# Bias-table groups, their loads and one tile size reordered in an attention-plus-MoE kernel

## The chip, the core and the metric

The kernel runs on one core of one Trainium2 chip. The metric is the device time of one execution in microseconds (us). The kernel before took 677.99 us, the median of 3 runs (677.85 to 678.35). Differences under about 0.2% (1.4 us) can't be told from no change here.

## The reference, cut to what matters

Attention with a learned position bias, over 4 batches, 8 heads, 576 positions and 64 values per head, feeds a mixture layer with a rational activation:

```python
scores = scale * np.matmul(q, k.transpose(0, 1, 3, 2))
psi_rel = np.log1p(np.abs(pos[:, None] - pos[None, :]))
psi_i = np.log1p(np.maximum(pos[:, None], 1.0))
h = np.maximum((psi_rel / psi_i)[..., None] @ w1 + b1, 0.0)   # 32 hidden
bias = h @ w2                                                 # one 576 x 576 table per head
attn = softmax(scores + bias.transpose(2, 0, 1))
x = (attn @ v).reshape(2304, 512)
hh = x @ w_in                                                 # 512 -> 2048
g = (a0 + a1*hh + a2*hh**2 + a3*hh**3) / (1 + |b0|*|hh| + |b1|*hh**2 + 1e-06)
out = g @ w_out                                               # 2048 -> 512
```

All is float32, and products of the mixture layer are made of a high and a low part of each operand (three matmuls in place of one).

## The kernel before, in words

**Table stage (0 to about 50 us).** The bias depends on the row position and the distance only, so it is built once, in 36 groups of 16 rows ("group n" holds rows 16n to 16n+15). For one group, VectorE (DVE) and ScalarE (ACT) make four relu rows in a ring of 18 buffers (line 614 on DVE, line 612 on ACT; how many of the four go to ACT depends on the group's width: none above 432 columns, one above 400, else two). TensorE (PE) multiplies them by the second weight (line 653, tile pb), ACT scales the result into a tile e (line 658, 8 buffers), and SyncE (SP) starts a DMA that writes it to a table in DRAM (line 664, tile tab). The relu rows are issued two groups ahead. The list `order` gives the order of the 36 groups; "place y" is a position in it, from 0 to 35.

Groups 0-7, 8-15, 16-23, 24-31 and 32-35 form blocks 0 to 4 of 128 rows (block 4: 64 rows). The function `load_bias(p, c)` (line 260) reads block c of head pair p back from DRAM into one row of a bias tile in SBUF with three DMAs (block 4: six, on 64 partitions each). It reads what line 664 wrote, so its first DMA waits in SP's queue until the block's last write has landed, and all that stands behind it in that queue waits with it. The dictionary `done` says after which place which block is loaded.

**Attention stage (about 46 to 270 us).** The work is cut into 72 steps. Step i computes scores of 128 rows for two heads on PE (line 337, tile sc), then DVE adds the bias and takes the minimum (line 347, two instructions a step; the first is row c of the bias tile of that step), ACT takes the exponential (line 363), PE transposes the result (line 406), ACT copies it (line 414), and PE multiplies by v (line 446). Two score tiles are shared by all steps, so PE can't begin the scores of a step before DVE has read those of the step before. The first steps, in order, use block 0, 1, 2 of unit 0, block 0, 1 of unit 1, then block 3 (step 5) and block 4 (step 6):

```python
steps = [(0, 0), (0, 1), (0, 2), (1, 0), (1, 1), (0, 3), (0, 4), (1, 2), (1, 3)]
```

The scores of steps 0 and 1 are issued at places 34 and 35 of the table stage (`EARLY = 2`). Unit 1's v is loaded by `load_v(1)` at place 21 and first used behind step 3. From step 4 on, weights are read and split into high and low parts in the gaps.

**Mixture stage (270 us to the end).** 48 steps of two matmul groups on PE: `x @ w_in` (line 313, tile h) and `g @ w_out` (line 787, tile o). Tiles of even token groups (xh, xl) lie in the pool xp on the right side of SBUF, those of odd token groups in a pool on the left side; of the four groups of weights in use, three lie in the pool wpool on the right side and the fourth (fp = 3) in a buffer of the bias pool, on the left.

The order on each engine is the order of the code (`tc.manual_schedule()`); no scheduler moves anything.

Of the kernel before, what the change touches and what calls it, by code (L numbers as in the profile page):

```python
# [8 lines left out]
F32 = mybir.dt.float32  # L9
# [7 lines left out]
P = 128  # L17
# [16 lines left out]
def tile_attn_moe(  # L34
# [14 lines left out]
    cpool = ctx.enter_context(tc.tile_pool(name="cpool", bufs=1))  # L49
# [16 lines left out]
    def tab_rows(c, h):  # L66
        n, w, o = P if c < 4 else 64, H * TW - 1, h * TW + S - 1 - P * c
        flat = tab[c].rearrange("r h x -> (r h x)")
        return flat[o:o + n * w].rearrange("(r w) -> r w", w=w)[:, :S]
# [11 lines left out]
        for d_, nm in ((woh, "woh"), (wol, "wol")):  # L81
            d_[g] = pool.tile([P, 2, DM], F32R, tag=f"{nm}{g}", name=f"{nm}{g}")

    fill = cpool.tile([P, 104], F32, tag="fill", name="fill")
    nc.gpsimd.memset(fill[:, 0:8], 0.0)
    stg = ctx.enter_context(tc.tile_pool(name="stg", bufs=2))
    bpool = ctx.enter_context(tc.tile_pool(name="bpool", bufs=2))
# [143 lines left out]
    with tc.manual_schedule():  # L231
# [3 lines left out]
        with ExitStack() as actx:  # L235
# [16 lines left out]
            def load_bias(p, c):  # L252
                if p not in bias:
                    bias[p] = bpool.tile([P, 10, S], F32, tag="bias", name=f"bias{p}")
                t = bias[p]
                r0, r1 = tab_rows(c, 2 * p), tab_rows(c, 2 * p + 1)
                for o, x, y, r in ((5 + c, 0, S, r1[:, 0:S]), (c, 64, S, r0[:, 0:512]), (c, 0, 64, r0[:, 512:S])):
                    n = P if c < 4 else 64
                    for z in range(0, P, n):
                        nc.sync.dma_start(out=t[z:z + n, o, x:y], in_=r)  # L260

            def load_qk(u, eng=nc.sync):
                p, b = units[u]
                q = qkp.tile([P, S], F32, tag="q", name=f"q{u}", bufs=3)
                k = qkp.tile([P, S], F32, tag="k", name=f"k{u}", bufs=3)
                eng.dma_start(out=q, in_=qt[b, p])
                eng.dma_start(out=k, in_=kt[b, p])
                qk[u] = (q, k)

            def load_v(u, eng=nc.sync):  # L270
                p, b = units[u]
                t = vpool.tile([P, 5, P], F32, tag="v", name=f"v{u}")
                eng.dma_start(out=t, in_=vp[b, p])
                vt[u] = t
# [292 lines left out]
            with ExitStack() as bctx:  # L567
                tpool = bctx.enter_context(tc.tile_pool(name="tpool", bufs=1, side="right"))
                rpool = bctx.enter_context(tc.tile_pool(name="rpool", bufs=8, side="right"))
                ring = [bpool.tile([P, 10, S], F32, tag="bias", name="ring")]  # L570
                ring = [ring[0][:, x, :] for x in range(10)]
                ring2 = tpool.tile([P, 8, S], F32, tag="ring2", name="ring2")
                ring += [ring2[:, x, :] for x in range(8)]
                lts = tpool.tile([P, S], F32, tag="lts", name="lts")
                bts = tpool.tile([P, NG * 4], F32, tag="bts", name="bts")
                LCUT = 320
                nc.scalar.dma_start(out=cs, in_=cst)
                nc.sync.dma_start(out=lts[:, :LCUT], in_=ltab[:, :LCUT])
                nc.sync.dma_start(out=lts[:, LCUT:], in_=ltab[:, LCUT:])
                for u in range(2):  # L580
                    load_qk(u)
                load_v(0)
                G.memset(qc, 1.0 + 1e-6)
                G.memset(wmin, -8.0 * 0x38000000)
                V.tensor_scalar(out=bts, in0=pts, scalar1=b1s, scalar2=None, op0=ALU.mult)
                A.activation(out=w28, in_=cs[:, 8 + 5 * NG:], func=AF.Identity, scale=8.0)
                for a, z in ((0, LCUT), (LCUT, S)):
                    V.tensor_scalar(
                        out=lts[:, a:z], in0=lts[:, a:z], scalar1=w1s, scalar2=None, op0=ALU.mult
                    )  # L590
                warm = ps_tp.tile([P, 2, 512], F32, tag="tp", name="warm")
                for x in range(9):
                    T.matmul(warm[:, 0, 0:P], ident, ident, start=True, stop=True)

                def dist(n):
                    return max(NROW * n + NROW, S - NROW * n)

                ENG = [
                    "DDDD" if dist(n) > 432 else "DDDA" if dist(n) > 400 else "DDAA" for n in range(NG)
                ]  # L600

                rows = {}
                LEAD, EARLY = 2, 2
                nring = [0]

                def relu(n):
                    for c, e in enumerate(ENG[n]):
                        r = ring[nring[0] % len(ring)][:, :dist(n)]
                        nring[0] += 1
                        m = 4 * n + c  # L610
                        if e == "A":
                            A.activation(out=r, in_=lts[:, :dist(n)], func=AF.Relu, bias=bts[:, m:m + 1])
                        else:
                            V.tensor_scalar(
                                out=r, in0=lts[:, :dist(n)], scalar1=bts[:, m:m + 1], scalar2=0.0,
                                op0=ALU.add, op1=ALU.max,
                            )
                        rows[n, c] = r

                bg = [w_job(f, z) for f in range(KF - LATE) for z in range(2)]  # L620
                after = {}
                for f in range(0 if wide else 6):
                    after[2 * f + 5] = [lambda f=f: [w_load(f, z) for z in range(2)]]
                after.setdefault(16, []).append(lambda: w_carve(3))
                for f in range(6, KH):
                    after[11 + f] = [lambda f=f: [w_load(f, z) for z in range(2)]]
                bg = in_order(bg, after)

                order = [16, 17, 0, 18, 1, 19, 2, 20, 3, 21, 4, 22, 5, 23, 6, 11, 7, 12]
                order += [8, 13, 32, 14, 33, 15, 34, 9, 35, 10, 31, 24, 30, 25, 29, 26, 28, 27]  # L630
                done = {16: 2, 19: 0, 30: 4, 31: 1}
                for n in order[:LEAD]:
                    relu(n)
                for y, n in enumerate(order):
                    if y == 21:
                        load_v(1)
                    if y + LEAD < NG:
                        relu(order[y + LEAD])
                    i0 = NROW * n
                    mid = i0 + NROW - 1  # L640
                    pool, nm = (ps_sc, "sc")
                    if y == NG - 1:
                        pool, nm = (ps_mx, "mx")
                    elif y % 3 == 1:
                        pool, nm = (ps_tp, "tp")
                    pa = pool.tile([P, 2, 512], F32, tag=nm, name=f"pb{n}")
                    cuts = sorted({0, mid, 512, EW})
                    for a, z in zip(cuts, cuts[1:]):
                        o = pa[:, a // 512, a % 512:a % 512 + z - a]
                        for c in range(4):  # L650
                            x = rows[n, c]
                            x = x[:, a - mid:z - mid] if a >= mid else x[:, mid - a:mid - z:-1]
                            T.matmul(
                                o[32 * c:32 * c + 32], w28[:, 32 * c:32 * c + 32], x,
                                start=True, stop=True,
                            )
                    e = rpool.tile([P, EW], F32, tag="e", name=f"e{n}")
                    A.activation(
                        out=e, in_=pa.rearrange("p a s -> p (a s)")[:, :EW], func=AF.Identity,
                        scale=rts[:, n:n + 1],  # L660
                    )
                    g, k = divmod(n, 8)
                    x0 = S - NROW - i0
                    nc.sync.dma_start(
                        out=tab[g][NROW * k:NROW * k + NROW, :, x0:x0 + EW].rearrange("r h x -> (r h) x"),
                        in_=e,
                    )
                    if y in done:
                        load_bias(0, done[y])
                    if y == NG - 1:  # L670
                        load_bias(0, 3)
                    if y >= NG - EARLY:
                        step_a(y - NG + EARLY)
                A.activation(out=babs, in_=abs_[:, 4:6], func=AF.Abs)
# [282 lines left out]
```

## Time and profile before

| | us |
|---|---|
| median of 3 runs | 677.99 (677.85 to 678.35) |
| the profiled execution, its own time | 679.69 |
| its span, first to last instruction | 677.9 |
| PE busy in the span | 667.6 (98%) |
| DVE busy | 570.6 (84%) |
| ACT busy | 481.9 (71%) |

The profiled execution is 1.70 us longer than the median of the runs, and 1.8 us of it lie outside the span. A row of a timeline gives the start and the length of a run of equal instructions and, in brackets, how long the engine was idle before it and what ended that. A row of stretches gives the length of the stretch and then, engine by engine, its busy time in it.

### The profile page before, as it was taken

How to read it: one execution, taken by the hardware profiler on the slowest of the kernel's cores; microseconds unless marked ns; L12 is line 12 of the kernel's file. 1: busy time of each engine (PE TensorE's matmuls, PEld its weight loads, DVE VectorE, ACT ScalarE, POOL GpSimd, SP SyncE). 2: the span in 40 equal slices, each digit the busy share in tenths (PEclk: the TensorE clock that was granted, in tenths of full speed). 3: DMA queues.
4: the chain of work that ended last, by engine and by line, in shares of the span. 5: the costliest groups of instructions: out<-in, count | busy, mean ns of one | idle time of the engine just before them, and what ended most of it. 6: DMA issues, size and time to landing. Idle time of an engine off the chain costs nothing.

```text
span 677.9 us, 16639 instructions
## 1 busy us (share of the span) xinstructions
PE 667.6 (98%) x6466; PEld 576.8 (85%) x6466; DVE 570.6 (84%) x1068; ACT 481.9 (71%) x769; POOL 156.5 (23%) x116
## 2 busy tenths in 40 slices
PE   9998999999999999999999999999999999999997
PEld 6766888888888888999999999999999999999995
DVE  7975788888888896699998989898978787878776
ACT  7976899998888997676676767676755555555561
POOL 0000034334333232122222222222222222222221
PEclk9998999999999999999999999999999999999999
DMA  6888488788788864223635353679721212122021
GB/s 241 287 303 304 159 279 275 224 284 258 245 262 291 270 217 141 98 81 115 221 98 203 90 191 99 199 217 358 251 104 47 94 47 93 47 94 94 1 94 46
DMA packets 74847, 119.01 MB, mean 176 GB/s; under 512 B 11905, under 2 KB 33809, under 8 KB 74769
## 3 DMA queue, kind: packets, MB, share of 16 engines
q1 hardware_dynamic: 74624, 117.79, 52.9%
q8 instruction: 51, 0.84, 0.5%
q14 instruction: 28, 0.22, 0.1%
q10 hardware_dynamic: 144, 0.16, 0.1%
HBM read 79.17 MB, written 35.61 MB: 169 GB/s over the span
## 4 chain that ended last, share of the span: by engine, by line
PE 91%; ACT 0%; DVEq 0%; issue 0%; DVE 0%; ACTq 0%
PE h L313 30%; PE o L787 29%; PE mx L446 13%; PE sc L337 12%; PE tp L406 5%; PE mx L406 1%; ACT pt L414 0%; PE mx L422 0%; DVEq L953 0%; ACT p L363 0%; DVE pre L808 0%; ACTq L414 0%
## 5 line engine op out<-in xcount | busy, mean ns | idle before, releaser
L756 POOL TENSOR_TENSOR gl<-m,r 128x768 fp32r<-128x768 f32 x47 | 87.2, 1855 | 309.6 <-DVE m L749 262.9
L347 DVE CUSTOM_DVE_ANT_0 s<-sc,bias 128x576 f32<-128x576 f32 x144 | 103.4, 753 | 16.9 <-PE sc L337 6.0
L709 ACT ACTIVATE w<-h,babs 128x768 f32<-128x768 f32 x48 | 43.3, 903 | 102.2 <-PE h L313 102.1
L363 ACT ACTIVATE p<-s,m 128x576 f32<-128x576 f32 x144 | 110.7, 772 | 5.2 <-DVE m L347 5.1
L313 PE MATMUL h<-xh,wih 128*128 128x384 f32 x288 | 97.0, 337 | 0.0
L337 PE MATMUL sc<-k,q 64*128 64x288 f32 (+1 forms) x640 | 92.6, 430 | 4.3 <-DVE m L347 4.3
L313 PE MATMUL h<-xh,wil 128*128 128x384 f32 x288 | 96.8, 336 | 0.0
L313 PE MATMUL h<-xl,wih 128*128 128x384 f32 x288 | 96.6, 336 | 0.0
L446 PE MATMUL mx<-pt,v 128*64 128x128 f32 (+1 forms) x1600 | 95.1, 267 | 0.0
L414 ACT COPY pt<-tp 128x1024 f32<-128x1024 f32 x72 | 72.5, 1007 | 25.7 <-PE tp L406 25.5
L787 PE MATMUL o<-wol,gh 128*128 128x512 f32 x216 | 85.5, 396 | 0.0
L787 PE MATMUL o<-woh,gh 128*128 128x512 f32 x216 | 85.0, 394 | 0.0
L446 PEld LDWEIGHTS mx<-pt,v 128*64 128x64 f32 x1600 | 78.5, 137 | 5.0 <-issue 0.2
L719 DVE SCALAR_TENSOR_TENSOR u<-w,babs,h 128x768 f32<-128x768 f32 x48 | 48.6, 1013 | 33.4 <-ACT t L710 33.4
L337 PEld LDWEIGHTS sc<-k,q 64*128 64x128 f32 (+1 forms) x640 | 50.4, 176 | 24.5 <-DVE m L347 11.1
L714 ACT ACTIVATE u<-u 128x768 f32<-128x768 f32 x48 | 40.7, 847 | 40.0 <-DVE u L719 40.0
L735 DVE SCALAR_TENSOR_TENSOR gh<-t,cst,r 128x768 fp32r<-128x768 f32 x48 | 48.7, 1015 | 9.5 <-ACT r L716 7.2
L787 PE MATMUL o<-woh,gl 128*128 128x512 f32 x216 | 56.2, 395 | 0.0
L313 PEld LDWEIGHTS h<-xh,wih 128*128 128x128 f32 x288 | 54.1, 188 | 1.9 <-issue 0.5
L313 PEld LDWEIGHTS h<-xl,wih 128*128 128x128 f32 x288 | 54.1, 188 | 1.5
L313 PEld LDWEIGHTS h<-xh,wil 128*128 128x128 f32 x288 | 54.1, 188 | 0.0
L742 DVE SCALAR_TENSOR_TENSOR m<-u,qc,gh 128x768 f32<-128x768 f32 x48 | 48.9, 1019 | 4.9
(73 smaller groups left out, 1266.5 us busy)
## 6 DMA issues: line engine op xcount, KB each, us to landing
tab<-e SPq DMA_DIRECT2D x36, 295.5 KB, 3.5
wx<-in_w_in_dram SPq DMA_DIRECT2D x16, 512.0 KB, 6.0
wx<-in_w_out_dram SPq DMA_DIRECT2D x16, 512.0 KB, 4.8
xr<-xd SPq DMA_DIRECT2D x7, 768.0 KB, 4.5
v<-in_vp_dram SPq DMA_DIRECT2D x16, 320.0 KB
ws<-wh SPq DMA_DIRECT2D x20, 256.0 KB, 2.0
ws<-wl SPq DMA_DIRECT2D x20, 256.0 KB, 3.9
q<-in_qt_dram SPq DMA_DIRECT2D x16, 288.0 KB
```

Source lines behind the costliest of these rows:

```text
L313: T.matmul(hps[s][:, j, :TT], w[:, k, sl], x[:, k, :], start=(k == 0 and z == 0), stop=(k == KD - 1 and z == 2),)
L337: T.matmul(sc[i, j][o, a, :SH], q[r, x], k[r, a * SH:(a + 1) * SH], start=True, stop=True,)
L347: V.tensor_tensor_reduce(out=t.rearrange("p (a s) -> p a s", a=2), in0=sc.pop((i, j))[:, :, :SH], in1=bias[p][:, 5 * j + c, :].rearrange(" ...
L363: A.activation(out=prob[i][:, z * S:z * S + S], in_=t, func=AF.Exp, bias=m, scale=-1.0, accum_out=sums[u % 4][:, k:k + 1],)
L414: A.copy(out=t[:, 0:8].rearrange("p x (r s) -> p r x s", r=2), in_=ps)
L446: T.matmul(ps[y, o], vt[n][:, kc, y], t[:, 2 * kc + j if kc < 4 else 8, o], start=(kc == 0), stop=(kc == 4),)
L709: A.activation(out=w, in_=h, func=AF.Abs, scale=babs[:, 1:2])
L719: V.scalar_tensor_tensor(out=et(s, "u", 2), in0=rt[s, "w"], scalar=babs[:, 0:1], in1=hps[s][:, :, :TT], op0=ALU.add, op1=ALU.mult,)
L735: V.scalar_tensor_tensor(out=hi, in0=rt[s, "t"], scalar=abs_[:, 0:1], in1=rt[s, "r0"], op0=ALU.add, op1=ALU.mult,)
L742: V.scalar_tensor_tensor(out=m, in0=rt[s, "u"], scalar=qc, in1=rt[s, "gh"].bitcast(F32), op0=ALU.add, op1=ALU.mult,)
L756: eng.tensor_tensor(out=lo, in0=rt[s, "m"], in1=rt[s, "r0"], op=ALU.mult)
L787: T.matmul(po[n, c], l[:, j, c * P:(c + 1) * P], r[fp][:, j, :], start=(first and x is a), stop=(last and x is z),)
```

## The change

The list of groups is changed from place 20 on: groups 9 and 10 move up next to 14 and 15, so that block 1 (groups 8 to 15) is complete at place 23 in place of 27, and the groups of block 4 (32 to 35) move from places 20, 22, 24, 26 to places 24, 26, 28, 30. Block 1 is loaded after place 26 in place of 31. Block 4 is loaded after block 3, behind place 35, in place of after place 30. `load_v(1)` is called at place 13 in place of 21. The tile `fill`, which nothing reads, grows from 104 to 112 columns, that is by 32 bytes in each partition; tiles of the pools on the left side that are laid behind it lie 32 bytes further up, those of the pools with `side="right"` stay.

```diff
-    fill = cpool.tile([P, 104], F32, tag="fill", name="fill")
+    fill = cpool.tile([P, 112], F32, tag="fill", name="fill")
...
                 order = [16, 17, 0, 18, 1, 19, 2, 20, 3, 21, 4, 22, 5, 23, 6, 11, 7, 12]
-                order += [8, 13, 32, 14, 33, 15, 34, 9, 35, 10, 31, 24, 30, 25, 29, 26, 28, 27]
-                done = {16: 2, 19: 0, 30: 4, 31: 1}
+                order += [8, 13, 9, 14, 10, 15, 32, 24, 33, 31, 34, 25, 35, 30, 26, 29, 28, 27]
+                done = {16: 2, 19: 0, 26: 1}
...
-                    if y == 21:
+                    if y == 13:
                         load_v(1)
...
                     if y == NG - 1:
                         load_bias(0, 3)
+                        load_bias(0, 4)
```

SP's queue before, in the last third of the table stage (e24 is the scaled tile of group 24, tab1 the table of block 1, bias0 the bias tile of head pair 0):

```order
L664 DMA tab1_67<-e10_737 128x591
L664 DMA tab3_69<-e31_757 128x591
L664 DMA tab3_69<-e24_777 128x591
L664 DMA tab3_69<-e30_797 128x591
L260 DMA bias0_511<-tab4_70 64x576 x2
L260 DMA bias0_511<-tab4_70 64x512 x2
L260 DMA bias0_511<-tab4_70 64x64 x2
L664 DMA tab3_69<-e25_823 128x591
L260 DMA bias0_511<-tab1_67 128x576
L260 DMA bias0_511<-tab1_67 128x512
L260 DMA bias0_511<-tab1_67 128x64
L664 DMA tab3_69<-e29_846 128x591
```

Block 1's load stands behind block 4's six DMAs and behind the write of place 31 (e25). SP's queue of the changed kernel, where block 1 is loaded now:

```order
L664 DMA tab1_67<-e15_657 128x591
L664 DMA tab4_70<-e32_677 128x591
L664 DMA tab3_69<-e24_697 128x591
L664 DMA tab4_70<-e33_717 128x591
L260 DMA bias0_513<-tab1_67 128x576
L260 DMA bias0_513<-tab1_67 128x512
L260 DMA bias0_513<-tab1_67 128x64
L664 DMA tab3_69<-e31_740 128x591
```

It stands behind the write of place 26 (e33), three writes behind the last one that it needs (e15), and nine writes stand behind it. SP's queue of the changed kernel at the end of the table stage:

```order
L664 DMA tab3_69<-e28_876 128x591
L664 DMA tab3_69<-e27_906 128x591
L260 DMA bias0_513<-tab3_69 128x576
L260 DMA bias0_513<-tab3_69 128x512
L260 DMA bias0_513<-tab3_69 128x64
L260 DMA bias0_513<-tab4_70 64x576 x2
L260 DMA bias0_513<-tab4_70 64x512 x2
L260 DMA bias0_513<-tab4_70 64x64 x2
L260 DMA bias1_956<-tab0_66 128x576
```

Block 4's six DMAs now stand behind block 3's load and ahead of the first load for head pair 1. ACT's queue before, from place 17's scaling (e12) on (ring and ring2 are the relu rows):

```order
L658 ACTIVATE e12_532<-pb12_519,cst_61 128x591
L658 ACTIVATE e8_552<-pb8_539,cst_61 128x591
L612 ACTIVATE ring2_131<-lts_132,bts_133 128x352 x2
L658 ACTIVATE e13_572<-pb13_559,cst_61 128x591
L658 ACTIVATE e32_595<-pb32_582,cst_61 128x591
L612 ACTIVATE ring_130<-lts_132,bts_133 128x336 x2
L658 ACTIVATE e14_617<-pb14_604,cst_61 128x591
L658 ACTIVATE e33_637<-pb33_624,cst_61 128x591
```

Here four relu rows lie among six scalings. ACT's queue of the changed kernel, the same stretch:

```order
L658 ACTIVATE e12_534<-pb12_521,cst_61 128x591
L612 ACTIVATE ring2_131<-lts_132,bts_133 128x432
L658 ACTIVATE e8_554<-pb8_541,cst_61 128x591
L612 ACTIVATE ring2_131<-lts_132,bts_133 128x352 x2
L658 ACTIVATE e13_574<-pb13_561,cst_61 128x591
L612 ACTIVATE ring_130<-lts_132,bts_133 128x416
L658 ACTIVATE e9_597<-pb9_584,cst_61 128x591
L612 ACTIVATE ring_130<-lts_132,bts_133 128x336 x2
```

Groups 9 and 10 put one relu row each on ACT (432 and 416 columns) where groups 32 and 33 put none, so six relu rows lie among four scalings there.

## Rows read from the trace of the kernel before

**Rows 1.** The page, busy time, share and instructions of each engine.

```profile
PE 667.6 (98%) x6466; PEld 576.8 (85%) x6466; DVE 570.6 (84%) x1068; ACT 481.9 (71%) x769; POOL 156.5 (23%) x116
```

**Rows 2.** Stretches: length, PE, PEld, DVE, ACT, POOL busy, granted clock, DMA share, GB/s.

```profile
40.00:44.00 4.00, 4.00 (x91) 2.80 (x87) 4.00 (x12) 3.36 (x5) 0.00 (x0) 1.00 1.01 376
48.00:52.00 4.00, 1.73 (x16) 0.99 (x8) 0.44 (x2) 2.12 (x5) 0.00 (x0) 1.00 0.76 221
52.00:56.00 4.00, 1.95 (x8) 1.38 (x10) 1.45 (x4) 1.72 (x5) 0.00 (x0) 0.79 0.82 317
56.00:60.00 4.00, 4.00 (x54) 3.23 (x52) 2.75 (x8) 2.06 (x4) 0.00 (x0) 0.79 0.65 184
...
180.00:220.00 40.00, 40.00 (x672) 33.56 (x670) 35.06 (x106) 36.05 (x71) 15.15 (x13) 1.00 0.87 278
```

**Rows 3.** Timeline of DVE, 47 to 69 us: start, us, instruction, [idle before].

```profile
47.00 0.76 DVE L347 CUSTOM_DVE_ANT_0 s<-sc,bias 128x576 f32<-128x576 f32 x1 [1.00 <-PE sc L337]
...
47.68 0.75 DVE L347 CUSTOM_DVE_ANT_0 s<-sc,bias 128x576 f32<-128x576 f32 x1
...
53.23 0.76 DVE L347 CUSTOM_DVE_ANT_0 s<-sc,bias 128x576 f32<-128x576 f32 x1 [4.78 <-DMA bias<-tab]
...
56.27 0.76 DVE L347 CUSTOM_DVE_ANT_0 s<-sc,bias 128x576 f32<-128x576 f32 x1 [1.60 <-ACT p L363]
...
58.89 0.76 DVE L347 CUSTOM_DVE_ANT_0 s<-sc,bias 128x576 f32<-128x576 f32 x1 [0.77 <-PE sc L337]
...
65.27 0.76 DVE L347 CUSTOM_DVE_ANT_0 s<-sc,bias 128x576 f32<-128x576 f32 x1 [0.76 <-ACT p L363]
...
68.20 0.76 DVE L347 CUSTOM_DVE_ANT_0 s<-sc,bias 128x576 f32<-128x576 f32 x1 [0.72 <-ACT p L363]
```

**Rows 4.** Timeline of SP's queue, 33 to 59 us.

```profile
33.87 8.56 SPq L664 DMA_DIRECT2D tab<-e  x10
43.97 4.05 SPq L260 DMA_DIRECT2D bias<-tab  x6
...
48.71 1.40 SPq L260 DMA_DIRECT2D bias<-tab  x3
50.20 2.16 SPq L664 DMA_DIRECT2D tab<-e  x4
56.26 2.69 SPq L260 DMA_DIRECT2D bias<-tab  x6
```

**Rows 5.** Timeline of PE, the scores of steps 0, 1 and 2.

```profile
45.73 1.24 PE L337 MATMUL sc<-k,q 64*128 64x288 f32 x8
...
48.04 1.69 PE L337 MATMUL sc<-k,q 64*128 64x288 f32 x8
54.05 2.48 PE L337 MATMUL sc<-k,q 64*128 64x288 f32 x7 [4.32 <-DVE m L347]
```

**Rows 6.** The stretch in which the granted clock is at half.

```profile
54.28:57.70 3.42, 3.42 (x27) 2.53 (x27) 1.70 (x5) 1.47 (x5) 0.00 (x0) 0.50 0.39 121
```

**Rows 7.** From issue to landing: table writes (line 664), all of them.

```profile
DMA to landing us min/median/max: 2.4/3.5/6.2
```

**Rows 8.** From issue to landing: bias loads (line 260), 0 to 90 us.

```profile
DMA to landing us min/median/max: 2.7/3.1/3.6
```

**Rows 9.** Timeline of ACT in the table stage.

```profile
32.62 0.76 ACT L612 ACTIVATE ring<-lts,bts 128x432 f32<-128x432 f32 x1
33.16 1.55 ACT L658 ACTIVATE e<-pb,cst 128x591 f32<-128x591 f32 x2
...
35.15 1.65 ACT L658 ACTIVATE e<-pb,cst 128x591 f32<-128x591 f32 x2
...
48.63 0.73 ACT L658 ACTIVATE e<-pb,cst 128x591 f32<-128x591 f32 x1
```

**Rows 10.** Stretches, line 313 alone: fp 3 of token group 0, fp 3 of group 1.

```profile
289.20:293.80 4.60, 4.40 (x24) 4.16 (x24) 1.00 0.00 0
...
322.60:327.20 4.60, 4.34 (x24) 4.17 (x24) 1.00 0.93 334
```

## The prediction

> **What bounds the kernel now.** I read the page first, for the engine that is never free. PE is busy for 667.6 of 677.9 us [rows 1], so only PE's few idle microseconds, and work that PE does slowly, can be won. Next I read the stretches, to find where they lie. From 180 to 220 us PE is busy in all 40.00 us; from 48 to 56 us it is busy for 1.73 and 1.95 of 4.00 us, and from 52 to 60 us the granted clock averages 0.79 in place of 1.00 [rows 2]. That is the seam between the table stage and the attention stage. Third I read DVE's timeline there, as PE waits for DVE: the first instruction of step 1 starts at 53.23 after 4.78 us of idleness, ended by a DMA into the bias tile [rows 3]. Step 1 reads block 1. Last I read SP's queue for why block 1 is late: its three DMAs are issued at 48.71, behind block 4's six, which hold the queue from 43.97 for 4.05 us [rows 4]. So the order in one queue holds up DVE, DVE holds the two score tiles, and PE stands idle for 4.32 us [rows 5]. Nothing waits for block 4 that early: it is first used in step 6, at 68.20 [rows 3].
>
> **The change part by part.** The sum is made on the profiled execution (span 677.9, own time 679.69) and taken off the median of 677.99; the two executions differ by 1.7 us outside what the change touches, and I carry the difference over unscaled.
>
> *Block 1 sooner.* When does its load land now? Its last group is at place 23. The scaling at that place started at 33.16 and may come 1.6 us later (below), so it ends by about 35.6 [rows 9]; its write is issued by 36.0 and lands 3.5 us later at the median, 6.2 at worst [rows 7], at 39.5 to 42.2. SP reaches the load behind place 26's write; that scaling, the second of the row at 35.15, ended at 36.80 [rows 9], or 37.9 with the 1.1 us that are left of the delay, so SP is there by 38.3 and then waits for the landing. Three DMAs took 1.40 us to issue [rows 4], and bias loads land 3.1 to 3.6 us after issue [rows 8]. Block 1 is there at 44.0 to 47.2. Step 1 can't use it so soon: its eight score matmuls run from 48.04 to 49.73, held by step 0's second DVE instruction, which ends at 48.43 [rows 3, 5]. In step 0 DVE starts at 47.00, right behind the eighth matmul (45.73 + 1.24 = 46.97). In step 1 only the second tile is held, and DVE's first instruction needs the first tile alone, so I put it a little ahead of the eighth, at 49.5. It was at 53.23: **3.7 us gained** (3.5 to 3.8).
>
> *The clock.* Behind PE's idle stretch the granted clock is 0.50 from 54.28 to 57.70, that is 1.2 in place of 2.4 GHz [rows 6]. It falls only behind the 4.32 us of idleness, and with them gone I expect it to stay at 1.00. What comes back is bounded by nothing and half of the 3.42 us, 1.7. From the start of step 1 to that of step 2 there are 3.04 us, from 2 to 3 there are 2.62 [rows 3]. At full clock steps 0 and 1 would stand 2.5 apart (47.00 and 49.5), the same chain of two DVE instructions and the scores. Twice 2.5 against 5.66 gives **0.7 us gained**.
>
> *The groups in another order.* The same 36 groups, with the same split over DVE and ACT, stay the same sum of work on DVE, ACT and PE, and the last two places are the same. But groups 9 and 10 each have a relu row on ACT, and 32 and 33 have none, and group 24, with two, comes four places sooner. ACT does the rows two places ahead, so at place 23's scaling it has done three rows more than before, at 0.54 us each (from 32.62 to 33.16 [rows 9]): 1.6 us late. At place 26 two rows are left of that, 1.1 us, and at the end none. DVE has no slack: it is busy in all of 40 to 44 us [rows 2], so what it loses there comes out at the end. What covers it is the ring: 18 buffers are 4.5 groups, the rows are issued 2 ahead, and 2.5 groups at about 1.0 us a place (33.16 to 35.15 for two [rows 9]) are 2.5 us, more than 1.6. I take **0.2 us lost** (0 to 1.6).
>
> *Block 4 later.* Its six DMAs leave the middle of the queue, where DMA was at a share of 1.01 [rows 2], and go behind block 3's. Place 35's scaling ends at 49.36 [rows 9]; written from 49.6 it lands at 53.1; block 3's three DMAs take 1.4, to 54.5, and land by 57.6, where step 5 comes at 65.27 - 4.2 = 61.1. Block 4's six take 2.7 (at the 0.45 of the row of six at 56.26) to 4.05 [rows 4], to 57.2 or 58.6, and land by 60.3 or 61.7; step 6 comes at 68.20 - 4.2 = 64.0. Cost nothing, with 3.5 and 2.3 us to spare. Behind them stand the next pair's first load, q and k of unit 2 and the weights, which lose the 2.7 us on the queue and gain about 3 from block 3's earlier start (56.26 to 53.1); none is used before step 8.
>
> *v of unit 1 at place 13.* One DMA moves out of the crowded stretch, where the ten writes from 33.87 take 8.56 us [rows 4]. At its new place it delays block 2's load at most by its own 0.43 us of issue and about 1 us of transfer (128 x 640 floats, 328 KB, at 317 to 376 GB/s [rows 2]), and block 2 is used in step 2, over 20 us later. Nothing.
>
> *32 bytes in `fill`.* Nothing is added; tiles on the left side move. The nearest rows for what a place can do: the same 24 matmuls take 4.40 us in fp 3 of token group 0 and 4.34 in fp 3 of group 1 [rows 10], and these differ in where xh and xl lie. Six of the 48 passes are of the slow kind: cured, 0.4 us are gained; if the other six passes of fp 3 turn slow, 0.4 are lost. I take 0, with 0.6 either way for all such effects.
>
> Sum: 3.7 + 0.7 - 0.2 = **4.2 us, 677.99 to 673.8** (profiled span about 673.7). With all terms at their bad ends it is 3.5 - 1.6 - 0.6 = 1.3, at their good ends 3.8 + 1.7 + 0.6 = 6.1; neither is likely, as the terms don't hang together. The likeliest case's own range is 672.7 to 674.8.
>
> **The rivals.** *Block 1 is still late.* For it: DMA is at a share of 1.01 where the load goes now, and the load waits for a write. If it met what stands at that end of the queue before (first DMA at 43.97, 4.05 us of issue, 3.1 to land), it would be there at 51.1, 1.6 after 49.5: 675.4. Against it: block 4's bytes and v have left the stretch, and with the worst landing 2.3 us are still left.
>
> *The wait moves to step 5 or 6.* With the worst landing (6.2), and issue at 0.68 a DMA, block 4 is there at 49.6 + 6.2 + 2.0 + 4.05 + 3.6 = 65.5, 1.5 after its step: 675.3. Against it: nine writes, spread over 41 to 49 us, leave DMA less behind than four in a burst from 50.20.
>
> *The clock still falls.* In steps 1 to 3 PE still pauses in each step for DVE to empty a score tile. No row here shows such short pauses with a lower clock: the only fall follows the long one. If it fell, the 0.7 us would not come back: 674.5. The Trainium skill, in "TensorE: Matmul & The Clock Gate" (section "A second HAM failure mode: psum-queue depth-cycling"), tells of a kernel whose frequent short pauses between groups of matmuls made the clock swing between half and full; that rule would bring this rival about, and the trace here neither shows nor excludes it.
>
> *Another limit gives the time back.* DMA is at a share of 0.87 from 180 to 220 us [rows 2]; were the end of the attention stage set by bytes and not by PE, all would be lost but what starts sooner: 677.9. Against it stands PE's 40.00 of 40.00 us there.
>
> *Slower: the tiles' new places.* If all of PE's work read from moved tiles slowed as fp 3 of group 0 does (0.06 of 4.34, 1.4%), some 600 us of it would cost 8.4 us: 677.99 - 4.2 + 8.4 = 682.2. It decides from 0.9% on (5.6 us). Against it: fp 3 of group 1 reads weights and activations from the left side, all of them tiles that move, and it is the quick one of the two [rows 10].
>
> **How the numbers follow.** Forecast 0.67; block 1 late 0.08; wait at step 5 or 6 0.07; clock 0.06; time given back 0.07; slower by placement 0.05. The range 672.6 to 675.9 holds the first four cases but their edges. 0.2% is 1.4 us, about what a measurement of this kernel can tell from no change: faster is the first four, 0.87, after 0.01 for edges; the same 0.08; slower 0.05.
>
> **What would show it.** Right: DVE's first instruction of step 1 near 49.5 with a wait for PE and not for a DMA; bias DMAs of block 1 issued at 39 to 42; no stretch at clock 0.50 before 60 us; step 3 near 54.5 and step 8 and all behind it 4.2 us sooner. Wrong: a wait for a bias DMA in step 1, 5 or 6; DVE's last relu row well past 46 us; matmuls of line 313 or 787 with other durations than before.

## The result, and the profile after

The changed kernel takes 672.52 us, the median of 6 runs (672.18 to 673.01). The kernel before took 678.50 us in 6 runs on the same chip (677.85 to 680.22). The ratio is 0.991, with a 95% interval of 0.9897 to 0.9922: faster by 6.0 us. The forecast was 673.8 and its range began at 672.6, so the direction was right and the gain was larger than the range allowed for. The profiled execution has a span of 671.2 us against 677.9, 6.7 us less.

The page of the changed kernel: busy time of each engine, the granted clock by slices, and the chain that ended last.

```profile
PE 664.9 (99%) x6466; PEld 575.3 (86%) x6466; DVE 570.3 (85%) x1068; ACT 481.7 (72%) x769; POOL 156.4 (23%) x116
...
PEclk9999999999999999999999999999999999999999
...
PE 99%; ACT 0%; issue 0%; DVEq 0%; DVE 0%; POOL 0%; ACTq 0%; POOLq 0%
```

PE's idle time fell from 10.3 us [rows 1] to 6.3, and PE is busy 2.7 us less with the same 6466 instructions. Those are two different gains, and the stretches part them. First the seam, columns as in [rows 2]:

```profile
48.00:52.00 4.00, 3.60 (x38) 2.20 (x31) 2.31 (x8) 3.72 (x9) 0.00 (x0) 1.00 0.80 301
52.00:56.00 4.00, 4.00 (x58) 3.08 (x57) 3.09 (x9) 3.19 (x8) 0.00 (x0) 1.00 0.39 121
```

PE works for 3.60 and 4.00 us where it worked for 1.73 and 1.95 [rows 2], and the clock is at 1.00. DVE's timeline of the changed kernel, the first instruction of steps 0, 1, 2, 3, 5 and 6, answers to [rows 3]:

```profile
47.42 0.76 DVE L347 CUSTOM_DVE_ANT_0 s<-sc,bias 128x576 f32<-128x576 f32 x1 [1.00 <-PE sc L337]
...
49.73 0.76 DVE L347 CUSTOM_DVE_ANT_0 s<-sc,bias 128x576 f32<-128x576 f32 x1 [0.87 <-PE sc L337]
...
52.14 0.76 DVE L347 CUSTOM_DVE_ANT_0 s<-sc,bias 128x576 f32<-128x576 f32 x1 [0.97 <-PE sc L337]
...
54.55 0.76 DVE L347 CUSTOM_DVE_ANT_0 s<-sc,bias 128x576 f32<-128x576 f32 x1 [0.76 <-PE sc L337]
...
60.94 0.76 DVE L347 CUSTOM_DVE_ANT_0 s<-sc,bias 128x576 f32<-128x576 f32 x1 [0.76 <-ACT p L363]
...
63.88 0.76 DVE L347 CUSTOM_DVE_ANT_0 s<-sc,bias 128x576 f32<-128x576 f32 x1 [0.72 <-ACT p L363]
```

The wait for a bias DMA is gone and none takes its place in steps 5 and 6. Step 1 comes 3.50 us sooner than before, step 3 4.34, and step 6 4.32 us. PE's scores of steps 0, 1 and 2 answer to [rows 5]; its pause of 4.32 us is one of 0.40:

```profile
46.15 1.24 PE L337 MATMUL sc<-k,q 64*128 64x288 f32 x8
...
48.46 1.69 PE L337 MATMUL sc<-k,q 64*128 64x288 f32 x8
...
50.55 1.67 PE L337 MATMUL sc<-k,q 64*128 64x288 f32 x7 [0.40 <-DVE m L347]
```

SP's queue of the changed kernel, against [rows 4]: v of unit 1, the writes, block 1's load, the writes behind it, and blocks 3 and 4 with the first load of the next pair.

```profile
22.97 0.43 SPq L273 DMA_DIRECT2D v<-in_vp_dram  x1
...
32.77 5.87 SPq L664 DMA_DIRECT2D tab<-e  x7
40.84 1.56 SPq L260 DMA_DIRECT2D bias<-tab  x3
42.44 7.69 SPq L664 DMA_DIRECT2D tab<-e  x9
53.44 6.57 SPq L260 DMA_DIRECT2D bias<-tab  x10
```

Block 1's load goes out at 40.84 in place of 48.71; its last DMA starts at 42.0 and lands 3.2 us later, 4.5 us before step 1 needs it.

That is the seam, 4.3 us. The second gain lies in the mixture stage, where the prediction put nothing. Against the kernel before, the mixture stage starts 4.25 us sooner and its last h pass 6.57 us sooner; the difference grows from step to step. The same instructions have become shorter. The page's groups of line 787 before, and of the same line after (it is line 788 there): instructions, busy time, mean ns of one.

```profile
L787 PE MATMUL o<-wol,gh 128*128 128x512 f32 x216 | 85.5, 396 | 0.0
L787 PE MATMUL o<-woh,gh 128*128 128x512 f32 x216 | 85.0, 394 | 0.0
L787 PE MATMUL o<-woh,gl 128*128 128x512 f32 x216 | 56.2, 395 | 0.0
```

```profile
L788 PE MATMUL o<-wol,gh 128*128 128x512 f32 x216 | 84.7, 392 | 0.0
L788 PE MATMUL o<-woh,gh 128*128 128x512 f32 x216 | 84.6, 392 | 0.0
L788 PE MATMUL o<-woh,gl 128*128 128x512 f32 x216 | 54.8, 389 | 0.0
```

Matmuls overlap, so the time that PE spends on a pass is read better from one pass's start to the next. PE's timeline before: the first matmul of an h pass of an even token group in fp 3, of the o pass behind it (fp 1, as the o passes run two steps behind), and of the next h pass.

```profile
289.33 0.34 PE L313 MATMUL h<-xh,wg 128*128 128x384 f32 x1
...
293.56 0.40 PE L787 MATMUL o<-woh,gh 128*128 128x512 f32 x1
...
297.77 0.34 PE L313 MATMUL h<-xh,wih 128*128 128x384 f32 x1
```

The same three matmuls in the changed kernel:

```profile
285.00 0.33 PE L313 MATMUL h<-xh,wg 128*128 128x384 f32 x1
...
289.18 0.39 PE L788 MATMUL o<-woh,gh 128*128 128x512 f32 x1
...
293.30 0.33 PE L313 MATMUL h<-xh,wih 128*128 128x384 f32 x1
```

The h pass takes 4.18 us in place of 4.23, the o pass 4.12 in place of 4.21. Below, the length of a pass is from the start of its first matmul to that of its last, in the traces (24 matmuls in an h pass, 18 in an o pass). The first and the last few steps, whose passes follow each other in another order, are left out of such ranges. Before, o passes take 3.95 to 3.97 us in fp 0 to 2 and 3.85 to 3.89 in fp 3, h passes 3.99 to 4.06. After, every o pass takes 3.894 and every h pass 4.013. Over 48 steps this is 36 o passes x 0.068 less, 12 of fp 3 x 0.022 more, 6 h passes x 0.05 less and 18 (odd groups, fp 0 to 2) x 0.013 more: about 2.3 us, and from its start to its last h pass the stage gains 2.32 (6.57 - 4.25).

### The profile page after: what moved, and what is told of

Its sections match the earlier page's. It is cut to its first block, busy times and chain, and to the rows that moved or that the text cites. A ratio compares the mean times of both kernels' runs of the same rounds, so it can differ in the third digit from the quotient of the medians.

```text
span 671.2 us, 16640 instructions
## 1 busy us (share of the span) xinstructions
PE 664.9 (99%) x6466; PEld 575.3 (86%) x6466; DVE 570.3 (85%) x1068; ACT 481.7 (72%) x769; POOL 156.4 (23%) x116
## 4 chain that ended last, share of the span: by engine, by line
PE 99%; ACT 0%; issue 0%; DVEq 0%; DVE 0%; POOL 0%; ACTq 0%; POOLq 0%
PE h L313 30%; PE o L788 29%; PE mx L446 13%; PE sc L337 13%; PE pb L653 6%; PE tp L406 5%; PE mx L406 1%; PE warm L593 1%; ACT pt L414 0%; PE mx L422 0%; DVEq L954 0%; ACT p L363 0%; DVE s L347 0%; POOL ident masks.py:199 0%; POOL ident masks.py:197 0%
## 5 line engine op out<-in xcount | busy, mean ns | idle before, releaser
L788 PE MATMUL o<-woh,gl 128*128 128x512 f32 x216 | 54.8, 389 | 0.0
```

Source lines behind the costliest of these rows:

```text
L788: T.matmul(po[n, c], l[:, j, c * P:(c + 1) * P], r[fp][:, j, :], start=(first and x is a), stop=(last and x is z),)
```

## The experiments

The change has two parts that lie far apart: the order (groups, loads, v) and the 32 bytes in `fill`. The first theory gives the seam to the order and the mixture stage to the bytes. Its rival gives all to the order, the mixture stage being quicker because the transfers of the weights come sooner.

**The order without the bytes, and the bytes without the order.** The first kernel is the changed one with one line back:

```diff
-    fill = cpool.tile([P, 112], F32, tag="fill", name="fill")
+    fill = cpool.tile([P, 104], F32, tag="fill", name="fill")
```

> The changed kernel with fill back at 104 columns: the new order of groups and loads alone. Theory A (two independent parts: about 4.3 us from the queue at the seam, seen in the traces as step 8 being 4.32 us sooner, and about 2.3 us from the 32 bytes in the mixture stage): span 673.6 to 673.8, 4.2 us under before, and the matmul passes of the mixture stage scatter as before (line 313 between 4.33 and 4.40 us, line 788 between 3.85 and 3.97 from first to last start). Theory B (the whole 6.7 us of the span come from the order, the mixture stage running better because it starts sooner): span near 671.2, passes as even as in the changed kernel.

It takes 674.76 us, ratio 0.9934 (0.992 to 0.9948) against 679.21 on the same chip. Step 1 starts at 49.57 with no wait for a DMA. The mixture stage's passes are those of the kernel before, 3.95 to 3.97 us for the o passes of fp 0 to 2 and 4.063 for the h pass of fp 3 in even groups, and so is the page's mean:

```profile
L788 PE MATMUL o<-wol,gh 128*128 128x512 f32 x216 | 85.5, 396 | 0.0
```

The second is the kernel before with only this line:

```diff
-    fill = cpool.tile([P, 104], F32, tag="fill", name="fill")
+    fill = cpool.tile([P, 112], F32, tag="fill", name="fill")
```

> The kernel before with fill at 112 columns and nothing else: the 32 bytes alone. Theory A: span 675.5 to 675.8, that is 2.2 to 2.4 us under before, all of it behind 270 us; every pass of line 313 and of line 787 takes the same time as in the changed kernel (4.013 and 3.894 us from first to last start); the wait of 4.78 us for block 1 stays. Theory B: span 677.9, no change.

It takes 676.95 us, ratio 0.9966 (0.9955 to 0.9977). The wait in step 1 stays, and the o passes are short. DVE's first instruction of step 1, and the page's row:

```profile
52.38 0.76 DVE L347 CUSTOM_DVE_ANT_0 s<-sc,bias 128x576 f32<-128x576 f32 x1 [3.85 <-DMA bias<-tab]
```

```profile
L787 PE MATMUL o<-wol,gh 128*128 128x512 f32 x216 | 84.7, 392 | 0.0
```

The two gains, 4.45 us (679.21 - 674.76) and 2.26 us (679.21 - 676.95), make 6.7. Taken off 679.21 that is 672.5, and the changed kernel took 672.52 us, and 672.61 in a second series (below): the gains add. The rival falls: 32 bytes that no instruction reads are worth a third of the gain. The profiled spans, one execution each, came out under what was expected, 672.9 and 675.2 us. In the first of them 0.55 us of the gain arises late, between steps 60 and 71 of the attention stage, and the cause of that was not looked for.

**What in the order is needed.** The kernel before, with block 4's load alone moved behind block 3's:

```diff
-                done = {16: 2, 19: 0, 30: 4, 31: 1}
+                done = {16: 2, 19: 0, 31: 1}
...
                         load_bias(0, 3)
+                        load_bias(0, 4)
```

> The kernel before with its old order of groups and fill at 104; only block 4's load is moved behind block 3's. Theory C (block 4's six DMAs ahead of block 1's in the queue were the wait): place 31's write goes out at about 43, place 27's lands by 44.5, block 1 is read from 44.5 and there at 49.0, so step 1 starts at 49.5 to 50 and the span is 673.7 to 674.3. Theory D (the groups of block 1 had to come sooner as well): block 1 lands at 51 or later, a wait of 1.5 us or more stays in step 1, span 675.3 or more.

It takes 674.80 us, ratio 0.9939 (0.9923 to 0.9955), as much as the whole order. SP's queue and DVE's first instruction of step 1:

```profile
44.30 2.44 SPq L260 DMA_DIRECT2D bias<-tab  x3
```

```profile
49.25 0.76 DVE L347 CUSTOM_DVE_ANT_0 s<-sc,bias 128x576 f32<-128x576 f32 x1 [0.87 <-PE sc L337]
```

Its span of 672.6 us is below the 673.7 that theory C expected at least. The six DMAs ahead of block 1 were the trouble; for this median neither the new order of the groups nor the sooner v was needed. One of the six runs takes 676.56 us, though, at a mean granted clock of 0.997 where the others have 0.999 or 1.000, so the wait may come back in some executions (that run has no trace). Next the opposite, the new order of the groups alone, the loads where they were:

```diff
-                order += [8, 13, 32, 14, 33, 15, 34, 9, 35, 10, 31, 24, 30, 25, 29, 26, 28, 27]
+                order += [8, 13, 9, 14, 10, 15, 32, 24, 33, 31, 34, 25, 35, 30, 26, 29, 28, 27]
```

> The kernel before with only the list of groups changed; loads stay after places 30 (block 4) and 31 (block 1), fill at 104. Block 4 is complete at place 30 itself now, so its load waits for a write that was only just issued. Theory C (the queue behind a load that waits is what costs): block 4's first DMA at 46 or later, block 1's at 50.5 to 51, landing at 54 to 55, so step 1 starts 1 to 2 us later than before: span 679 to 680. Theory D (the sooner groups are what helps): step 1 no later than before, span 677.9 or less.

It takes 681.70 us, ratio 1.0038 (1.0022 to 1.0053): slower than before, and by more than was expected. SP's queue (block 4's load, then block 1's), DVE's step 1, and the stretch that follows:

```profile
46.66 3.72 SPq L260 DMA_DIRECT2D bias<-tab  x6
...
51.04 1.40 SPq L260 DMA_DIRECT2D bias<-tab  x3
```

```profile
55.67 0.76 DVE L347 CUSTOM_DVE_ANT_0 s<-sc,bias 128x576 f32<-128x576 f32 x1 [7.20 <-DMA bias<-tab]
```

```profile
56.00:60.00 4.00, 3.51 (x26) 3.09 (x27) 2.21 (x7) 1.72 (x5) 0.00 (x0) 0.50 0.47 162
```

Block 4's last group stands at place 30 in that order, and its load behind the same place: SP waits there for the landing of the write that it has just issued, and block 1 waits behind it. DVE's idle stretch is 7.20 us in place of 4.78 [rows 3], PE's is 6.74 in place of 4.32, and a clock of 0.50 follows it again. The order of the groups is worth something only with the loads put to fit it.

**The smallest change with both gains.** Block 4 last and 32 bytes, the old order of groups:

```diff
-    fill = cpool.tile([P, 104], F32, tag="fill", name="fill")
+    fill = cpool.tile([P, 112], F32, tag="fill", name="fill")
...
-                done = {16: 2, 19: 0, 30: 4, 31: 1}
+                done = {16: 2, 19: 0, 31: 1}
...
+                        load_bias(0, 4)
```

> The kernel before with its old order of groups, block 4's load behind block 3's, and fill at 112 columns: the two parts that carried the gain, without the new order of groups and without the sooner v. If the parts add (theory A) and the new order of groups is worth nothing (theory C): step 1 at 49.2 to 49.4, passes of the mixture stage at 4.013 and 3.894 us, span 670.2 to 670.8, at or just under the changed kernel. If the new order of groups is worth something after all: span over 671.5.

It takes 672.58 us, ratio 0.9897 (0.9878 to 0.9916) against 679.66. The changed kernel itself was run once more beside it:

> The changed kernel once more, beside the run above on the same chip: span 670.4 to 671.2 as before; the run above should be the same or up to 0.5 us shorter.

It takes 672.61 us, ratio 0.9894 (0.9873 to 0.9914). The two can't be told apart. But the smaller change has no slack in step 1, as its profiled execution shows, whose span of 671.3 us is longer than the 670.2 to 670.8 expected:

```profile
50.29 0.76 DVE L347 CUSTOM_DVE_ANT_0 s<-sc,bias 128x576 f32<-128x576 f32 x1 [1.75 <-DMA bias<-tab]
```

PE's pause ahead of the scores of step 2 is 1.28 us there:

```profile
51.11 1.67 PE L337 MATMUL sc<-k,q 64*128 64x288 f32 x7 [1.28 <-DVE m L347]
```

The load of block 1 goes out at 43.91 and, among the writes, lands too late in this execution; in the kernel with block 4 last and 104 columns, which issues at about the same time, it did not. What the new order of the groups buys is slack: its load goes out some 3 us sooner, at 40.84 against 43.91 and 44.30. That this slack is worth time is not shown by the medians.

**Why 32 bytes count.** The first question is whether the left side's place counts by itself. The changed kernel with the left side 32 bytes further up, and 64:

```diff
-    fill = cpool.tile([P, 112], F32, tag="fill", name="fill")
+    fill = cpool.tile([P, 120], F32, tag="fill", name="fill")
```

> The changed kernel with fill at 120 columns: the tiles on the left side lie 32 bytes further up again, so that they begin 32 bytes off a multiple of 64, as in the kernel before, but at other addresses. Theory E (what counts is whether tiles begin at a multiple of 64 bytes): passes scatter exactly as before the change (line 313: 4.063 in fp 3 of even token groups, else 3.99 to 4.013; line 788: 3.95 to 3.97 in fp 0 to 2), span 672.9 to 673.5. Theory F (the particular addresses of the changed kernel count, multiples of 256 for many tiles): passes differ from both kernels.

```diff
-    fill = cpool.tile([P, 112], F32, tag="fill", name="fill")
+    fill = cpool.tile([P, 128], F32, tag="fill", name="fill")
```

> The changed kernel with fill at 128 columns: the tiles on the left side lie 64 bytes further up than in the changed kernel, again at multiples of 64 but most of them no longer at multiples of 128 or 256. Theory E: passes as in the changed kernel (4.013 and 3.894 us), span 670.4 to 671.2. Theory F: the passes scatter, span 672 or more.

They take 675.35 and 674.35 us (one run each, as are all that follow), and their passes scatter again, though not as in the kernel before: o passes of 3.956 to 3.963 us (but for one with a pause in it) and of 3.958 to 3.967 in fp 0 to 2. Theory E, which expected the old lengths of the first and the good ones of the second, falls. The page's rows of the first and of the second:

```profile
L788 PE MATMUL o<-wol,gh 128*128 128x512 f32 x216 | 85.4, 395 | 0.0
```

```profile
L788 PE MATMUL o<-wol,gh 128*128 128x512 f32 x216 | 85.3, 395 | 0.0
```

So neither any shift does it, nor every place at a multiple of 64 bytes from the good one. Next both sides moved together: `fill` at 104 columns, and on the right side the unused tile `edge` grown by 32 bytes, so that the two sides lie to each other as in the changed kernel.

```diff
-    fill = cpool.tile([P, 112], F32, tag="fill", name="fill")
+    fill = cpool.tile([P, 104], F32, tag="fill", name="fill")
...
-            G.memset(wpool.tile([P, 120], F32, tag="edge", name="edge"), 0.0)
+            G.memset(wpool.tile([P, 128], F32, tag="edge", name="edge"), 0.0)
```

> The changed kernel with fill back at 104 columns, and the unread tile edge of the right side 32 bytes larger (128 for 120 columns), so that the right side's tiles lie 32 bytes lower too: all tiles of both sides are 32 bytes below their places in the changed kernel. Theory G (what counts is how the two sides lie to each other): the passes are even as in the changed kernel (4.013 and 3.894 us), span 670.4 to 671.2. Theory H (what counts is where a tile begins by itself, at a multiple of 256 or more): the passes scatter as before the change or more, span 672.9 or more.

It takes 672.63 us, and every h pass takes 4.013 and every o pass 3.894 us again. The first matmuls of an h pass, an o pass and the next h pass: 4.19 and 4.12 us.

```profile
284.54 0.33 PE L313 MATMUL h<-xh,wg 128*128 128x384 f32 x1
...
288.73 0.39 PE L788 MATMUL o<-woh,gh 128*128 128x512 f32 x1
...
292.85 0.33 PE L313 MATMUL h<-xh,wih 128*128 128x384 f32 x1
```

The distance between the sides counts, not where either of them lies by itself. If so, it should be the two tiles that one matmul reads, and single tiles can be moved to show it. With `fill` at 104 and an unused tile of 32 bytes ahead of the mixture stage's own pools, gh, gl and the odd groups' xh and xl lie as in the changed kernel, and only the weights of fp 3 lie 32 bytes off:

```diff
-    fill = cpool.tile([P, 112], F32, tag="fill", name="fill")
+    fill = cpool.tile([P, 104], F32, tag="fill", name="fill")
...
+            gap = mctx.enter_context(tc.tile_pool(name="gap", bufs=1, reuse_waits="tile"))
+            gap.tile([P, 8], F32, tag="gap", name="gap")
```

> The changed kernel with fill at 104 columns and an unused 32-byte tile ahead of the mixture stage's own pools: their tiles (gh, gl, odd xh and xl) lie as in the changed kernel, the fourth group of weights (fp 3) 32 bytes lower, as before the change. Theory I (a pass is slow by the pair of tiles that it reads): passes of fp 0 to 2 as in the changed kernel (4.013 and 3.894 us), passes of line 313 in fp 3 at 4.063 in all 12 token groups, line 788 in fp 3 other than 3.894; span about 671.4 to 671.9. Rival: passes of fp 0 to 2 scatter too.

The reverse is the changed kernel with the unused tile and `fill` at 112: the weights of fp 3 at their good place, the mixture stage's own tiles 32 bytes off.

```diff
+            gap = mctx.enter_context(tc.tile_pool(name="gap", bufs=1, reuse_waits="tile"))
+            gap.tile([P, 8], F32, tag="gap", name="gap")
```

> The changed kernel with an unused 32-byte tile ahead of the mixture stage's own pools: weights of fp 3 and the attention stage lie as in the changed kernel, gh, gl and odd xh, xl 32 bytes further up. Theory I: line 788 at 3.95 to 3.97 us in all four fp, since all weights now lie otherwise than gh and gl; line 313 near 4.00 to 4.01 throughout; span 673.5 to 674.3. Rival: only fp 0 to 2 change.

They take 673.73 and 675.85 us, the first with a span of 672.0 just over the 671.4 to 671.9 expected. In the first, the passes of fp 0 to 2 are the short ones (o 3.894, h 4.012 to 4.019) and those of fp 3 the long ones (o 3.957, h 4.063). In the second, all o passes are long (3.956 to 3.963). The same three matmuls (line 787 is line 790 here) in the first, 4.25 us for the h pass of fp 3 and 4.12 for the o pass of fp 1, and in the second, 4.19 for each:

```profile
284.13 0.34 PE L313 MATMUL h<-xh,wg 128*128 128x384 f32 x1
...
288.38 0.39 PE L790 MATMUL o<-woh,gh 128*128 128x512 f32 x1
...
292.50 0.33 PE L313 MATMUL h<-xh,wih 128*128 128x384 f32 x1
```

```profile
285.13 0.33 PE L313 MATMUL h<-xh,wg 128*128 128x384 f32 x1
...
289.32 0.39 PE L790 MATMUL o<-woh,gh 128*128 128x512 f32 x1
...
293.51 0.34 PE L313 MATMUL h<-xh,wih 128*128 128x384 f32 x1
```

For the o passes theory I holds in every placement that was run. By the tile addresses in the kernels, those whose activations and weights begin at the same place modulo 256 bytes take 3.85 to 3.90 us, all others 3.95 to 3.97. gh and gl share their pool with the tiles on which DVE, ACT and POOL work, and moved together with these, so that for the o passes these runs don't part the tiles that the matmul reads from the work tiles beside them.

For the h passes the two tiles don't decide alone. The long kind of 4.06 us comes up only where they begin at different places modulo 256 bytes, but not in all such passes. With `fill` at 120, two h passes of one odd group, fp 1 and fp 2, whose tiles lie alike modulo 256 bytes, take 4.16 and 4.24 us from start to start (3.987 and 4.063 in length):

```profile
301.72 0.34 PE L313 MATMUL h<-xh,wih 128*128 128x384 f32 x1
305.88 0.63 PE L788 MATMUL o<-wg,gh 128*128 128x512 f32 x2
310.01 0.34 PE L313 MATMUL h<-xh,wih 128*128 128x384 f32 x1
314.25 0.39 PE L788 MATMUL o<-woh,gh 128*128 128x512 f32 x1
```

What else counts there stays open. Last, whether the effect repeats: the left side 256 bytes lower than in the changed kernel.

```diff
-    fill = cpool.tile([P, 112], F32, tag="fill", name="fill")
+    fill = cpool.tile([P, 48], F32, tag="fill", name="fill")
```

> The changed kernel with fill at 48 columns: the left side lies 256 bytes lower than in the changed kernel, the right side where it was. If what counts repeats after 256 bytes (theory G or H with a period of 256 or less): passes as in the changed kernel, span 670.4 to 671.2. If the period is longer: the passes scatter, span 672 or more.

It takes 672.97 us with all passes at 4.013 and 3.894, as the row of the page says too:

```profile
L788 PE MATMUL o<-wol,gh 128*128 128x512 f32 x216 | 84.7, 392 | 0.0
```

After 256 bytes the two sides stand well again; 32 bytes to either side of the good place, and 64 above it, they don't. In the three placements with even passes the operand tiles of all passes begin at the same place modulo 256 bytes. A shift by 128 bytes was not tried.

## Why the prediction was right at the seam and wrong in the sum

*Block 1 sooner* (3.7 us): right. The load went out at 40.84, forecast 39.5 to 42.2, and landed at about 45.2, forecast 44.0 to 47.2. Step 1 started at 49.73 behind PE's scores, forecast 49.5: 3.50 us gained. The rival in which block 1 is still late fell with it: DVE waits for PE there, and not for a DMA.

*The clock* (0.7 us): right. No stretch at 0.50 follows step 1, the steps come 2.41 us apart, and at step 3 the gain is 4.34 us, 0.84 more than at step 1. The short pauses that a rival feared, 0.40 us on PE and 0.76 to 0.97 on DVE, left the granted clock at 1.00. So did PE's pause of 1.28 us in the smaller change. PE's pauses of 3.38 us (the bytes alone), 4.32 (before) and 6.74 (the groups alone) were each followed by 0.50. The Trainium skill tells of a kernel whose frequent short pauses made the clock swing ("TensorE: Matmul & The Clock Gate", section "A second HAM failure mode: psum-queue depth-cycling"). No such swing followed the few pauses here.

*The groups in another order* (0.2 us lost): about right, and not settled. Step 0 came 0.42 us late in the changed kernel, 0.26 in the one without the bytes, but only 0.02 with the groups alone, so executions differ by as much as the term. *Block 4 later* and *v* (nothing): right; steps 5 and 6 wait for ACT, and the steps behind are 4.32 us sooner, forecast 4.2. At the end of the attention stage 4.25 of it is left, so the rival in which another limit gives the time back fell too.

*32 bytes in `fill`* ("I take 0, with 0.6 either way for all such effects"): this is the step that failed. It is worth 2.3 us by the traces and 2.26 by the runs. I had priced it by the h passes alone, and of these by the slow kind of fp 3, 6 of 48: that part gave 0.3 where 0.4 was said, and 18 other h passes gave 0.2 of it back. I had not read the o passes. Their two kinds stood in the trace of before, 3.95 to 3.97 us in fp 0 to 2 and 3.85 to 3.89 in fp 3, and line 787 has 36 passes of the slow kind, each with activations on the left and weights on the right. Read by the same rule as the h passes, cured they were 36 x 0.07 = 2.5 us, and 673.8 less 2.5 is 671.3, below the range. The trace of before could not settle it alone, as the o passes of fp 3 also take their matmuls in another order (the function `mm2` sorts those of fp 0 to 2); after the change both orders take 3.894, so the order was not the cause. The rival *slower by placement* had seen that PE's time can hang on the tiles' places and gave it one sign only; the runs show a scatter of passes between a short and a long kind, and the kernel before stood on the long side.

*The base*: "the two executions differ by 1.7 us outside what the change touches" was wrong too. The kernel before takes 677.53 to 680.54 us in 18 runs of one chip. The 8 runs with a mean granted clock of 0.996 or 0.997 take 677.53 to 678.86, the 10 with 0.994 or 0.995 take 679.11 to 680.54. With the order alone, at a clock of 0.999 or 1.000, it is 674.42 to 674.92, and the changed kernel takes 672.18 to 673.01 in 12 runs, while the one with the bytes alone, which still waits, has 675.64 to 678.16. So the spread goes with the clock, and most likely lay in the wait and the slow stretch behind it, the very thing removed; only one execution of each kernel has a trace, so that this is not shown. The fast 677.99 had less to give than the average execution: the order alone ends at 674.76, 3.2 us under 677.99 and not 4.2. The sum was thus about 1.0 us too low for the seam and left out 2.2 for the bytes, two errors of opposite sign. That 672.52 lies only 0.08 us outside the range is luck.

## What to carry to other kernels

A DMA that must wait for a write's landing holds all that stands behind it in its queue: order such loads by when they are first used, and put none ahead of one that is needed sooner. Where an engine is busy for 98%, look at the lengths of equal passes before costing a change of tile places at nothing: if they come in two kinds, multiply the difference by the count of every pass of the long kind. And if runs of a kernel spread more than those of its relatives, the spread may lie in the very wait that is to go.

## What was not expected of the hardware

The same matmuls on the same data take 3.894 or up to 3.97 us a pass (o), 4.013 or up to 4.064 (h), by how the tiles of the two sides lie to each other in SBUF. Here 32 bytes decide, and after 256 bytes it repeats. For the o passes it goes with the stationary and the moving tile of the pass, for the h passes not with these alone. A pass of the short kind can even be shorter still (h 3.99, o 3.85), but then others are long, and of the placements that were run with block 1 in time the three with even passes had the lowest times (672.5 to 673.0 us). What in TensorE or SBUF makes the difference the traces don't show, and it stays open.
